# w_q's sixteen-partition block, and the last 128 columns of two weight loads, moved from SyncE's DMA queue to GpSimd's

## The chip, the cores and the metric

The kernel runs on one core of a Trainium2 chip. The metric is the device time of one launch in microseconds. It is the median of several runs; the kernel before has 376.38 us (three runs, 376.34 to 377.0).

## The reference, cut to what matters

One decode step for two rows of x (448 wide). The row is normalised; an attention branch with a cached K and V (8 key-value heads, 16 query heads, 4096 positions of 256) and a feed-forward branch read the normalised row; the second gates the first.

```python
xn = _layernorm(x)                                  # x: 2 x 1 x 448
q = xn @ wq                                         # 448 x 4096
p = softmax(q @ k.T * 256 ** -0.5)                  # k, v: 2 x 8 x 4096 x 256
s = (p @ v) @ wo                                    # wo: 4096 x 448
h = (xn @ w_gate) * (xn @ w_up)                     # 448 x 1792 each
return x + s * silu(h @ w_down)                     # w_down: 1792 x 448
```

Everything is float32. The caches and the weights are some 158 MB, and each byte is used once.

## The kernel before, in words

The kernel is one long stream of loads with the arithmetic beside it. `plan()` (L82) lists the loads in order and `issue()` (L62) sends the next ones. All of them go through SyncE's queue (L75, L79), in this order: `wq0` (half of w_q, 128 partitions x 6656 columns), its extra block `wqx`, `first` (K of the first of 16 batch-head pairs), then fourteen loads `vk[i]` of 8 MB (V of pair i and K of pair i + 1), and among them three loads of weights: `wgu` (w_gate and w_up, 12544 columns) after vk[0], `wdq` (w_down and the other half of w_q, 13440 columns) after vk[2], and `wo` after vk[8]. The last pair's loads `last0` and `last1` are cut into ten pieces. K and V share a ring of two buffers, and all weights one buffer (`slot`), so a load's issue waits until the matmuls that read the buffer's former contents are done.

`wqx` stands for a part of w_q that the kernel takes out of the regular fold. w_q has 448 rows: three blocks of 128 and 64 more. For `wq0` half of those last 64 rows' columns lie on partitions 64 to 127 of the regular load; the other half, 256 KB, is `wqx`: 16 partitions x 4096 columns, read from an array whose outer dimension is 4 (`wqx[:, :4]`, L79; L413 to L415). In `rows()` (L165), which computes x @ w, L173 multiplies the three full blocks, L179 the sixteen-partition block, and L182 or L186 the rest. `query(h)` (L191) turns the result into qT.

Ahead of the first query x is loaded by one DMA of ScalarE's queue (L102), VectorE normalises it (L114 to L124) with one power by GpSimd (L120), TensorE transposes it (L127, L138) with an identity that GpSimd has made.

For each pair, `scores(i)` (L245) multiplies q by K; `softmax` and `over` (L246 to L270) make the transposed weights; `values(i)` (L277) multiplies them by V. The order is written by hand (the pool's scheduler is off): values(i), scores(i + 1), then the issue of the next loads, then the softmax. The feed-forward part (`ffn_in`, L213; `ffn_out`, L223), the second query and the projection by wo (`project`, L301) are put in after pairs 0, 2, 4 and 8. At the end `project_last` (L307) multiplies the last pieces of wo, which come behind the last V in `last1`, and L380 to L382 gate, add and store.

Of the kernel before, what the change touches and what calls it, by code (L numbers as in the profile page):

```python
# [13 lines left out]
B, D = 2, 448  # L14
# [6 lines left out]
FC = F // NT  # L21
KB = 16
ROW = 8192
# [5 lines left out]
PART = 14 * (D + 512)  # L29
SIDE = 16  # L30
EXTRA = 8
EPS = 1e-5


# [2 lines left out]


@with_exitstack
def gated_decode_block(ctx: ExitStack, tc: tile.TileContext, x, first, vk, last0, last1, wq0, wqx, wdq, wo, wgu, out):  # L40
    nc = tc.nc
    ring = ctx.enter_context(tc.tile_pool(name="ring", bufs=2))
    slot = ctx.enter_context(tc.tile_pool(name="slot", bufs=1))
# [5 lines left out]
    def bank(name="t", bufs=1):  # L49
        return psum.tile([128, 512], F32, name=name, bufs=bufs)  # L50
# [8 lines left out]
    loaded = {}  # L59
    todo = []  # L60

    def issue(n=1):  # L62
        for names, src, cuts in todo[:n]:
            weight = names[0].startswith("w")
            if weight:
                t = slot.tile([128, PART], F32, name="slot", align_bytes=512)
            else:
                t = ring.tile([128, 2 * ROW], F32, name="ring", align_bytes=512)
            width = ROW if not weight else src.shape[1] // len(names)
            for i, name in enumerate(names):  # L70
                loaded[name] = t[:, i * width:(i + 1) * width]
            if names == ["wd", "wq1"]:
                loaded["wd"], loaded["wq1"] = t[:, :14 * D], t[:, 14 * D:]
            for lo, hi in zip(cuts, cuts[1:]):
                nc.sync.dma_start(t[:, lo:hi], src[:, lo:hi])  # L75
            if names == ["wq0"]:
                at = src.shape[1]
                loaded["wqx"] = t[:, at:at + EXTRA * 512]
                nc.sync.dma_start(loaded["wqx"][:SIDE], wqx[:, :4])  # L79
        del todo[:n]  # L80

    def plan(names, src, cuts=None):  # L82
# [9 lines left out]
    plan(f"k{LAST + 1} v{LAST}", last0, [0, ROW, 2 * ROW])  # L92
    plan(f"v{LAST + 1} wo2", last1, [0, 4096, 7168, *(ROW + i * D // 2 for i in (0, 6, 12, 14, 15, 16))])
    issue(3)


# [2 lines left out]

    e0, e1 = early()  # L100
    x2 = e0[:, 0, :D]
    nc.scalar.dma_start(x2, x)  # L102
    ident = const.tile([128, 128], F32)
    make_identity(nc, ident)
    one = const.tile([1, 1], F32)
# [11 lines left out]
    nc.vector.scalar_tensor_tensor(sq, xc, 1.0, xc, op0=OP.mult, op1=OP.mult, accum_out=st[:, 2:3])  # L117
    nc.vector.tensor_scalar(st[:, 3:4], st[:, 2:3], 1.0 / D, EPS, op0=OP.mult, op1=OP.add)
    rstd = const.tile([B, 1], F32)
# [16 lines left out]
    for j in range(NK):  # L136
        at = 384 + j * SIDE
# [65 lines left out]
    def lift(ps):  # L203
        t = work.tile([128, D], F32, name="h")
        nc.scalar.copy(t, ps[:, :D])
        return t
# [42 lines left out]
    def softmax(s, m, pT=None):  # L249
        sm = bank("sm", 1)  # L250
        nc.tensor.transpose(sm[:1, :128], m[:, 0:1], ident)  # L251
        mx = work.tile([1, NT, W], F32, name="mx", bufs=1)
        nc.vector.tensor_reduce(  # L253
            mx, sm[:1, None, :128].rearrange("p o (c j) -> p o j c", c=NT).to_broadcast([1, NT, W, NT]),
            axis=AX.X, op=OP.max)
        nc.tensor.transpose(sm[:, 128:129], mx.rearrange("p c j -> p (c j)"), one)  # L256
        nc.vector.tensor_scalar(m[:, 1:2], sm[:, 128:129], -1.0 / 16, None, op0=OP.mult)  # L257
        su = work.tile([128, 2], F32, name="su")
        p = work.tile([128, 2, 512], F32, name="p", bufs=1)
        nc.scalar.activation(p, s, AF.Exp, bias=m[:, 1:2], scale=1.0 / 16, accum_out=su[:, 0:1])  # L260
        if pT is None:
            pT = work.tile([128, 2, 512], F32, name="pT", bufs=1)
        nc.vector.transpose(pT.rearrange("p h n -> p (h n)"), p.rearrange("p h n -> p (h n)"))  # L263
        return pT, su, sm

    def over(p):

        pT, su, sm = p
        nc.tensor.matmul(sm[:, 130:131], add_head.rearrange("p a r j -> p (a r j)"), su[:, 0:1], start=True, stop=True)  # L269
        nc.vector.reciprocal(su[:, 1:2], sm[:, 130:131])  # L270
        return pT, su[:, 1:2]
# [48 lines left out]
    oT2 = const.tile([128, 1, 2, REP, W], F32)  # L320
    ss = scores(0)
    issue(2)
    p = over(softmax(*ss))
    for i in range(LAST):
        g, b = divmod(i, B)
        o = bank("o", 1)
        values(i, p[0], o)
        ss = scores(i + 1)

        issue(1 + (i + 1 in weights))  # L330
        nc.scalar.activation(ob[:, b * 4 + g if g < 4 else b * 3 + g - 4], o, AF.Copy, scale=p[1])  # L331
        if i == LAST - 1:
            cb = combine(ob, 6)
        p = softmax(*ss)
        if i < LAST - 1:
            p = over(p)
        if i == 7:
            cb = combine(ob, 8)
            for n in range(B):
                turn(oT0, cb[:, n * 256:(n + 1) * 256], 0, n, 4)  # L340
            ob = work.tile([128, 8, 512], F32, name="ob", bufs=1)
        if i in (0, 2, 4, 8):
            if i == 0:
                ffn_in()
            if i == 2:
                ffn_out()
            if i == 4:
                query(1)
            if i == 8:
                project(oT0, 0, 0, EARLY)  # L350
# [6 lines left out]
    t = lift(wide)  # L357

    last = slot.tile([128, PART], F32, name="slot", align_bytes=512)
    p = softmax(*ss, last[:, :1024].rearrange("p (h n) -> p h n", h=2))  # L360
    o = bank("o", 1)
# [5 lines left out]
    o = bank("wide", 1)  # L367
# [66 lines left out]
```

## Time and profile before

| what | value |
|---|---|
| median of 3 runs | 376.38 us (376.34 to 377.0) |
| the profiled execution's own time | 376.44 us |
| its span, first to last instruction | 374.7 us |
| TensorE matmul busy | 209.0 us (56% of the span) |
| VectorE, ScalarE, GpSimd busy | 63.2, 36.3, 1.2 us |
| bytes moved by DMA | 158.79 MB, 424 GB/s over the span |

The profile is of one execution. Its lines give start and length in us from the span's start. A load's line stands at its issue on SyncE's queue ("SPq") and not where its bytes move; the share of DMA is the mean over the core's 16 DMA engines. [...] A share can be a few hundredths above 1, since a packet is counted where it starts.

### The profile page before, as it was taken

What the parts mean: (1) busy time and instruction counts of PE and PEld (TensorE: products, weight loads), DVE (VectorE), ACT (ScalarE), POOL (GpSimd) and SP (SyncE); (2) the same over time, 40 slices, a digit from 0 to 9 for tenths busy, and PEclk for the clock granted to TensorE, in tenths of its full rate; (3) what the DMA queues carried; (4) which work ended last, traced back from release to release, by engine and by line L of the source; (5) the groups of instructions that cost most, each with busy time, mean ns of one, the idle gap of its engine ahead of it and who ended that gap; (6) DMA issues with size and microseconds to landing.
All of it is one profiled execution on the core that took longest, in us unless ns stands there. A gap on an engine that the chain in (4) does not pass through costs nothing.

```text
span 374.7 us, 3272 instructions
## 1 busy us (share of the span) xinstructions
PE 209.0 (56%) x1472; PEld 63.0 (17%) x1472; DVE 63.2 (17%) x113; ACT 36.3 (10%) x56; POOL 1.2 (0%) x7
## 2 busy tenths in 40 slices
PE   1792468174736092869174666641718191909795
PEld 0110112021211020212021112210202020202232
DVE  4003021103030003030303030300211203020431
ACT  1001010001012002010101010100010101010120
POOL 1000000000000000000000000000000000000000
PEclk9968586657686567789758687865968776877899
DMA  8999899999999999999999999999999999999994
GB/s 322 438 500 434 374 439 448 441 443 435 425 429 448 441 441 393 429 448 436 427 448 434 436 422 409 444 448 434 441 428 429 441 441 406 450 409 434 415 418 181
DMA packets 4357, 158.79 MB, mean 424 GB/s; under 512 B 614, under 2 KB 1000, under 8 KB 1384
## 3 DMA queue, kind: packets, MB, share of 16 engines
q1 hardware_dynamic: 4340, 158.59, 98.2%
q8 instruction: 11, 0.18, 0.2%
q10 hardware_dynamic: 4, 0.00, 0.0%
q14 instruction: 2, 0.02, 0.0%
HBM read 158.54 MB, written 0.06 MB: 423 GB/s over the span
## 4 chain that ended last, share of the span: by engine, by line
DMA 76%; PE 22%; issue 0%; SPq 0%; DVE 0%
DMA ring<-vk 67%; PE o L277 11%; PE s L245 8%; DMA ring<-last 6%; DMA slot<-wq 3%; PE t L179 1%; PE t L173 1%; PE t L182 1%; SPq L75 0%; PE acc L313 0%; DVE qT L195 0%; DVE h L380 0%; DVE h L381 0%
## 5 line engine op out<-in xcount | busy, mean ns | idle before, releaser
L277 PE MATMUL o<-ring,pT 128*32 128x512 f32 x480 | 83.1, 855 | 91.5 <-DMA ring<-vk 91.5
L245 PE MATMUL s<-ring,qT 128*32 128x512 f32 x512 | 61.8, 624 | 2.4 <-ACT p L260 1.5
L246 DVE TENSOR_REDUCE m<-s 128x1 f32<-128x1024 f32 x16 | 19.6, 1225 | 222.1 <-PE s L245 222.1
L277 PEld LDWEIGHTS o<-ring,pT 128*32 128x32 f32 x480 | 21.2, 149 | 143.6 <-issue 142.0
L331 ACT ACTIVATE ob<-o,su 128x512 f32<-128x512 f32 x14 | 9.6, 688 | 190.7 <-PE o L277 190.7
L260 ACT ACTIVATE p<-s,m 128x1024 f32<-128x1024 f32 x16 | 17.8, 1114 | 97.5 <-DVE m L257 97.5
L245 PEld LDWEIGHTS s<-ring,qT 128*32 128x32 f32 x512 | 18.0, 115 | 44.6 <-issue 40.4
L263 DVE STREAM_TRANSPOSE pT<-p 128x1024 f32<-128x1024 f32 x15 | 18.7, 1245 | 21.2 <-ACT p L260 21.2
L269 PE MATMUL sm<-su,add_head 128*128 128x1 f32 x32 | 7.6, 305 | 22.9 <-ACT p L260 22.9
L251 PE MATMUL sm<-ident,m 128*1 128x128 f32 x16 | 4.3, 270 | 18.9 <-DVE m L246 18.8
L253 DVE TENSOR_REDUCE mx<-sm 1x128 f32<-1x512 f32 x16 | 10.8, 678 | 6.3 <-PE sm L251 6.3
L173 PE MATMUL t<-slot,xnT 128*32 128x512 f32 x48 | 8.8, 887 | 3.4 <-DMA slot<-wq 3.4
L269 PEld LDWEIGHTS sm<-su,add_head 128*128 128x128 f32 x32 | 6.2, 242 | 25.4 <-ACT p L260 24.1
L256 PE MATMUL sm<-one,mx 1*128 1x1 f32 x16 | 3.5, 218 | 12.3 <-DVE mx L253 12.3
L304 PE MATMUL wide<-slot,oT 128*32 128x448 f32 x48 | 7.2, 759 | 0.0
L173 PE MATMUL s<-slot,xnT 128*32 128x448 f32 x48 | 7.2, 748 | 0.1
L227 PE MATMUL t<-slot,hT 128*32 128x448 f32 x28 | 5.6, 911 | 2.4 <-DMA slot<-wdq 2.4
L251 PEld LDWEIGHTS sm<-ident,m 128*1 128x1 f32 x16 | 1.3, 79 | 33.0 <-DVE m L246 32.3
L286 PE MATMUL cb<-ob,add_blocks 128*32 128x64 f32 (+2 forms) x64 | 5.6, 475 | 0.8 <-ACT ob L372 0.8
L179 PE MATMUL t<-slot,oT 16*32 16x512 f32 x16 | 5.7, 703 | 0.0
L195 DVE STREAM_TRANSPOSE qT<-t 128x256 f32<-128x256 f32 x4 | 1.6, 428 | 19.8 <-PE t L179 15.2
L256 PEld LDWEIGHTS sm<-one,mx 1*128 1x128 f32 x16 | 2.1, 133 | 15.4 <-DVE mx L253 15.4
(71 smaller groups left out, 54.1 us busy)
## 6 DMA issues: line engine op xcount, KB each, us to landing
ring<-last SPq DMA_DIRECT2D x2, 4096.0 KB, 24.8
slot<-wdq SPq DMA_DIRECT2D x1, 6720.0 KB
slot<-wgu SPq DMA_DIRECT2D x1, 6272.0 KB, 34.3
slot<-wo SPq DMA_DIRECT2D x1, 5376.0 KB, 40.9
ring<-first SPq DMA_DIRECT2D x1, 4096.0 KB, 21.4
slot<-wq SPq DMA_DIRECT2D x1, 3328.0 KB, 10.7
ring<-last SPq DMA_DIRECT2D x1, 2048.0 KB, 14.7
ring<-last SPq DMA_DIRECT2D x1, 1536.0 KB
```

Of the source, the lines that this page charges most:

```text
L173: nc.tensor.matmul(ps[W * c:W * (c + 1), :n], xnT[:, k, :], block(NT * k + c), start=k == 0, stop=False)
L179: nc.tensor.matmul(ps[W * c:W * (c + 1), :n], xeT[:, j, :], extra[:SIDE, at:at + n], start=False, stop=j == NK - 1)
L227: nc.tensor.matmul(ps[W * t:W * (t + 1), :D], hT[:, i], loaded["wd"][:, i * D:(i + 1) * D], start=i < NT, stop=i >= 14 - NT)
L245: nc.tensor.matmul(s[W * c:W * (c + 1), h, :], q[:, d], k[:, h, d, c, :], start=d == 0, stop=d == 1)
L246: nc.vector.tensor_reduce(m[:, 0:1], s, axis=AX.XY, op=OP.max)
L253: nc.vector.tensor_reduce(mx, sm[:1, None, :128].rearrange("p o (c j) -> p o j c", c=NT).to_broadcast([1, NT, W, NT]), axis=AX.X, op=OP.max)
L260: nc.scalar.activation(p, s, AF.Exp, bias=m[:, 1:2], scale=1.0 / 16, accum_out=su[:, 0:1])
L263: nc.vector.transpose(pT.rearrange("p h n -> p (h n)"), p.rearrange("p h n -> p (h n)"))
L269: nc.tensor.matmul(sm[:, 130:131], add_head.rearrange("p a r j -> p (a r j)"), su[:, 0:1], start=True, stop=True)
L277: nc.tensor.matmul(o[W * t:W * (t + 1), :], pT[:, h, at:at + 2 * W:2], loaded[f"v{i}"][:, e * 512:(e + 1) * 512], start=e < NT, stop=e >= ...
L304: nc.tensor.matmul(wide[W * t:W * (t + 1), :D], heads(oT, i, first), loaded["wo"][:, i * D:(i + 1) * D], start=i < NT, stop=i >= LATE - NT)
L331: nc.scalar.activation(ob[:, b * 4 + g if g < 4 else b * 3 + g - 4], o, AF.Copy, scale=p[1])
```

## The change

`wqx` is loaded by GpSimd's queue and not by SyncE's. The arrays `wgu` and `wdq` lose their last 128 columns, which move into an array `ends`; where these two loads are issued, GpSimd's queue loads the 128 columns in six parts, of 17, 17, 17, 19, 29 and 29 partitions. Each row of a part is two pieces of 64 numbers (256 B), which in `ends` lie 16 numbers apart from each other. x is loaded by two DMAs of one row each, still on ScalarE's queue. Nothing else is changed: what is computed, from which buffers, and the order of all other instructions stay.

```diff
+END = 128
+PARTS = [0, 17, 34, 51, 70, 99, 128]
...
-            width = ROW if not weight else src.shape[1] // len(names)
+            width = ROW if not weight else 28 * FC // len(names)
...
             for lo, hi in zip(cuts, cuts[1:]):
                 nc.sync.dma_start(t[:, lo:hi], src[:, lo:hi])
+            if names in (["wg", "wu"], ["wd", "wq1"]):
+                at = src.shape[1]
+                for lo, hi in zip(PARTS, PARTS[1:]):
+                    nc.gpsimd.dma_start(t[lo:hi, at:at + END].rearrange("p (o n) -> p o n", o=2),
+                                        ends[names[0] == "wd", lo:hi, :, :END // 2])
             if names == ["wq0"]:
                 at = src.shape[1]
                 loaded["wqx"] = t[:, at:at + EXTRA * 512]
-                nc.sync.dma_start(loaded["wqx"][:SIDE], wqx[:, :4])
+                nc.gpsimd.dma_start(loaded["wqx"][:SIDE], wqx[:, :4])
...
-    nc.scalar.dma_start(x2, x)
+    for b in range(B):
+        nc.scalar.dma_start(x2[b:b + 1], x[b:b + 1])
...
+    ends = np.zeros((2, 128, 2, END // 2 + 16), np.float32)
+    for i, w in enumerate((wgu, wdq)):
+        ends[i, :, :, :END // 2] = w[:, -END:].reshape(128, 2, END // 2)
+    wgu, wdq = c(wgu[:, :-END]), c(wdq[:, :-END])
```

More of the change, by code (lines that the diff above doesn't have):

```diff
@@ L31, with gated_decode_block @@
 EXTRA = 8
+END = 128
+PARTS = [0, 17, 34, 51, 70, 99, 128]
 EPS = 1e-5
 @with_exitstack
-def gated_decode_block(ctx: ExitStack, tc: tile.TileContext, x, first, vk, last0, last1, wq0, wqx, wdq, wo, wgu, out):
+def gated_decode_block(ctx: ExitStack, tc: tile.TileContext, x, first, vk, last0, last1, wq0, wqx, wdq, wo, wgu, ends, out):
     nc = tc.nc
@@ L423 @@
     wdq = np.concatenate([wd, wq1], 1)
+    ends = np.zeros((2, 128, 2, END // 2 + 16), np.float32)
+    for i, w in enumerate((wgu, wdq)):
+        ends[i, :, :, :END // 2] = w[:, -END:].reshape(128, 2, END // 2)
+    wgu, wdq = c(wgu[:, :-END]), c(wdq[:, :-END])
     nc = bacc.Bacc("TRN2", target_bir_lowering=False, num_devices=1, dynamic_dma_scratch_size=1024)
-    arrays = dict(x=x, first=first, vk=vk, last0=last[0], last1=last[1], wq0=wq0, wqx=wqx, wdq=wdq, wo=wo, wgu=wgu)
+    arrays = dict(x=x, first=first, vk=vk, last0=last[0], last1=last[1], wq0=wq0, wqx=wqx, wdq=wdq, wo=wo, wgu=wgu, ends=ends)
     args = [nc.dram_tensor(n, a.shape, mybir.dt.from_np(a.dtype), kind="ExternalInput").ap()
```

## The prediction, made before the changed kernel was run

> **What bounds the kernel now.** I read the page first: its DMA line, its queues, its chain.
>
> ```profile
> span 374.7 us, 3272 instructions
> DMA  8999899999999999999999999999999999999994
> q1 hardware_dynamic: 4340, 158.59, 98.2%
> q8 instruction: 11, 0.18, 0.2%
> DMA 76%; PE 22%; issue 0%; SPq 0%; DVE 0%
> ```
>
> The 16 DMA engines are busy in every slice but the last, 98.2% of the span with SyncE's queue, q1. So the kernel is a stream of bytes, and the chain names DMA for 76%. The pace of one engine follows: 158.59 MB in 0.982 x 16 x 374.7 = 5887 us is 26.9 GB/s. With all engines full, the time can move in three ways only: a gap in the stream, more or fewer bytes (here none), or a different sharing of the bytes among the 16 engines, for the slowest engine sets the end. The change touches the third, so the next view is the stretch table of the last microseconds (column before the last: the engines' mean busy share).
>
> ```profile
> 367.25:367.75 0.50, 0.50 (x6) 0.00 (x0) 0.00 (x0) 0.00 (x0) 0.00 (x0) 1.00 1.05 406
> 367.75:368.75 1.00, 0.21 (x6) 0.03 (x5) 0.00 (x0) 0.69 (x1) 0.00 (x0) 1.00 0.73 281
> 368.75:369.25 0.50, 0.50 (x28) 0.50 (x32) 0.03 (x1) 0.00 (x0) 0.00 (x0) 1.00 0.66 244
> 369.25:370.25 1.00, 0.53 (x24) 0.32 (x20) 0.22 (x1) 0.00 (x0) 0.00 (x0) 1.00 0.45 165
> 370.25:370.50 0.25, 0.25 (x13) 0.25 (x17) 0.00 (x0) 0.00 (x0) 0.00 (x0) 1.00 0.35 118
> 370.50:370.75 0.25, 0.25 (x20) 0.25 (x15) 0.00 (x0) 0.00 (x0) 0.00 (x0) 1.00 0.15 50
> 370.75:371.00 0.25, 0.25 (x19) 0.17 (x8) 0.00 (x0) 0.00 (x0) 0.00 (x0) 1.00 0.04 14
> ```
>
> All 16 work until about 367.7; then they stop one after another, and 0.35 x 16 = 5 to 6 of them work beyond 370.25, the last to about 370.9. Work left after 367.75 is 0.73 + 0.33 + 0.45 + 0.09 + 0.04 + 0.01 = 1.65 us on all sixteen, so with a perfect sharing it would end at 369.4. **No sharing can gain more than 1.5 us** (0.4%).
>
> Does the end follow the last bytes? The chain's end says so:
>
> ```profile
> 348.98 21.08 DMA ring<-last
> 370.06 0.14 issue
> 370.19 1.45 PE acc L313 x48
> ```
>
> L313 waits for a piece that lands at 370.06 and then runs at its own pace to the end. An earlier landing is followed at once, as far as about 0.6 us: L313 also needs a VectorE transpose, which ends at 369.47.
>
> ```profile
> 369.22 0.25 DVE L296 STREAM_TRANSPOSE oT<-cb 128x64 f32<-128x64 f32 x1 [2.99 <-PE cb L286]
> ```
>
> That transpose hangs on the last V, whose landing moves with the same engines. So I count the stream's end one to one.
>
> **Who is late?** wqx tells of four engines.
>
> ```profile
> 0.74 10.72 DMA slot<-wq
> 2.48 0.44 SPq L75 DMA_DIRECT2D ring<-vk  x1
> SPq L75 <- DMA slot<-wqx: 10.9, 1, 10.9
> ```
>
> wq has landed at 11.46. SyncE, free at 2.92, waits 10.9 us for wqx: landed at 13.8, 2.4 us behind wq. Its 256 KB on all sixteen engines are 16 KB each, 0.61 us; on four they are 64 KB each, 2.43 us. So four engines carry wqx, and start the long stream 2.4 us behind. The other delays are q8's: 0.2% of 16 x 374.7 = 12 us (9 to 15 by the rounding) for 11 packets of 16 KB, **0.8 to 1.4 us each**, where q1 takes 0.61. Of the 5 to 6 late engines at most four are those of wqx; at least two others end within half a microsecond of the last.
>
> **The change part by part.**
>
> *SyncE's two shorter loads.* Each engine carries 8 rows of a 128-row load. Each row loses 512 B, in two loads: 2 x 8 x 512 B / 26.9 GB/s = **0.30 us less on every engine**.
>
> *The twelve parts.* The same 128 KB come back on GpSimd's queue as 256 B pieces. The price of a small piece, from the tail:
>
> ```profile
> DMA packets 627, 1.33 MB, mean 252 GB/s; under 512 B 81, under 2 KB 465, under 8 KB 626
> q1 hardware_dynamic: 626, 1.32, 63.9%
> ```
>
> This is the stretch 366 to 371.3: 0.639 x 16 x 5.3 = 54.2 us for 1.32 MB, which at the pace are 49.1. The 5.1 us left are 8 ns for each of 626 packets. A piece of 256 B is then 9.5 + 8 = 18 ns if it is a packet by itself, 9.5 ns if its neighbours share one. A part of 17 rows is 34 pieces, 0.32 to 0.60 us; 19 rows 0.36 to 0.67; 29 rows 0.55 to 1.02. No row of GpSimd's queue exists before. If a part is spread over all engines it is nothing in balance (8 rows out, 8 in, up to +0.3). If it is on one engine, that engine has the whole price. I take one engine for each part: wqx went to four, which divides its outer counts 16 and 4, and 17, 19 and 29 are divisible by no smaller number. With 4 + 6 + 6 = 16 shares, I take each engine to get one: wqx's four no part, the other twelve one each. Then wqx's four end 0.30 us sooner, eight engines gain 0.02 to 0.30 (19 rows: 0.37), four gain 0.25 to 0.72.
>
> [...]
>
> *The handover.* q8's packets cost 0.2 to 0.8 us over their 0.61: an engine that takes a packet of another queue loses something. For a part on GpSimd's queue I bound this by 0 and 0.8, and take **0.2**: q8's packet is 16 KB, a part only 8.7. For wqx, four rows of 16 KB an engine, the bound is 0 to 4 x 0.8 = 3.2; I take 0.2, as one handover, because GpSimd's first packets run against a queue that is just filling, and keep the upper end as a rival.
>
> *wqx beside wq.* It no longer stands behind wq but beside it, so wq's last rows on the four engines land up to 2.4 us later. L173 waits for them:
>
> ```profile
> 11.60 4.28 PE t L173 x24
> 23.32 0.33 SPq L75 DMA_DIRECT2D slot<-wgu  x1
> SPq L75 <- DMA ring<-vk: 12.6, 1, 12.6
> ```
>
> The query, and with it the issue of wgu at 23.32, slide to 25.8. What hides it: the queue still holds vk[0], whose landing SyncE awaits from 30.24 for 12.6 us, to 42.8. Cover 19.5 us, slide 2.4: nothing. The same cover takes what GpSimd's issue of wqx puts ahead of the identity and of the power at L120 (nearest rows below: 0.79 us for wqx on SyncE; in this trace GpSimd issues none), and x's second DMA (0.53 us on ScalarE):
>
> ```profile
> 0.74 0.53 ACTq L102 DMA_DIRECT2D p<-x  x1
> 1.18 0.79 SPq L79 DMA_DIRECT2D slot<-wqx  x1
> 8.23 0.25 ACT L149 COPY xg<-t 128x112 f32<-128x112 f32 x1 [5.64 <-PE t L146]
> ```
>
> The normalisation's chain is through at 8.2, 3.4 us ahead of L173. SyncE's `first` and vk[0] issue 0.8 us earlier into a queue that is full: no gain.
>
> *The new waits.* GpSimd's first part waits for the weight buffer as SyncE's wgu does, and five parts queue behind it; nothing else is on GpSimd's queue after L120, so nobody waits there. The readers:
>
> ```profile
> 65.67 0.96 PE L186 MATMUL s<-slot,xnT 64*32 64x448 f32 x8
> 66.69 0.33 SPq L75 DMA_DIRECT2D slot<-wdq  x1
> 168.91 1.06 PE L186 MATMUL t<-slot,xnT 64*32 64x512 f32 x8
> ```
>
> wgu's last columns are read by the last L186 at 65.67, 40 us after the parts are issued; wdq's by 168.91, 102 us after 66.69. Six issues even of 2 us each are hidden many times. If this cover were gone, L186 would hold TensorE, not the stream, until the next ring buffer came free late.
>
> **The sum.** Before, the last engine ends at 370.93 at the latest, the late ones that are not wqx's at 370.3 to 370.7. Afterwards: wqx's at 370.63 (+0.2 for a handover: 370.8); the others at 370.5 + 0.30 + 0.2 = 371.0, between 370.3 and 371.9. I take 371.1, since some late engine may be one with 19 or 29 rows: **+0.2 us**. The profiled execution's 376.44 becomes 376.6; it lay 0.06 above the median, so 376.6 stands for the median too. Own range 376.0 to 377.1. About 0.2% (0.75 us) is what a measurement of this kernel can tell from no change.
>
> **The rivals.**
>
> 1. *The crossing of wqx costs per row* (slower). Every 16 KB row of wqx alternates with a row of wq and costs what a q8 packet does, 0.2 to 0.8 more. Four such on engines that are already last: 4 x 0.5 - 0.30 = +1.7 us, **378.1**, up to 379.3. It decides beyond 0.26 us a row (1.05 / 4). For it: q8's row. Against: q1's own packets follow one another at full pace, and a queue with work waiting need not behave as one that wakes up. 18%.
> 2. *wqx goes to other engines than the four* (slower). If GpSimd's shares begin elsewhere, 2.43 us fall on an engine that is late for another reason: 370.5 - 0.30 + 2.43 = 372.6, +1.7, **378.1**; on engines delayed less, +0.7. Nothing in the trace says where GpSimd's shares begin. 10%.
> 3. *Small pieces cost double* (slower). The pieces of 256 B take 36 ns and not 18: 34 of them 1.2 us, the late engine +0.9, with the handover 371.6, +0.7 to +0.9, **377.2**. 7%. [...]
> 4. *wqx lands on the engines that finish first* (faster). From 367.75 to 368.75 a quarter of the engines is done already. 2.43 us there end by 370.4, its former four drop out, and the late others end at 370.3 to 370.7, less 0.30, plus a part if it is shared finely: **375.6 to 376.1**; the bound of all sharing is 374.9. 10%.
> 5. The forecast: the shares move by tenths of a microsecond and mostly cancel. 55%.
>
> **How the numbers follow.** Slower by over 0.2%: 18 + 10 + 7 = 35%. Faster by over 0.2%: 10%. Within 0.2%: 55%. The range takes in both signs' cheaper halves: 375.7 to 378.4.
>
> **What would show it.** In the profile after: GpSimd's queue as a row of its own with some 0.4 MB; q1 with fewer bytes; L173 at up to 14 us; wgu issued near 25.8, and the DMA line full at 20 to 45 us all the same. In the tail's stretch table the busy share should fall more steeply and later, with fewer engines in the 368s idle, and the last packet within 0.5 us of 370.9. wqx landing much later than 13.8, or an end beyond 371.9, speaks for rival 1 or 2; GpSimd's share of time above 0.4 MB at 26.9 GB/s (15 us, 0.25%) plus 16 x 0.2 us prices the handover. The prediction is wrong if the stream has a gap anywhere before 367, or if the number of engines that end late is set by something that I have not seen.

## The result and the profile after

The changed kernel takes 399.24 us (median of four runs, 398.61 to 399.6), beside 376.37 before: 1.0601 times as long, with a 95% interval of 1.0587 to 1.0614. That is **22.9 us slower**. The forecast was 376.6, and the whole range (375.7 to 378.4) misses it. The profiled execution took 399.51 us, its span 397.8 is 23.1 longer than before.

The page of the changed kernel, first its busy line of DMA and its queues:

```profile
span 397.8 us, 3311 instructions
DMA  8999999993699999999909999999999999999995
q1 hardware_dynamic: 4320, 158.20, 93.3%
q0 software_dynamic: 912, 0.42, 0.5%
DMA 45%; issue 35%; PE 17%; POOL 3%; SPq 0%; DVE 0%; POOLq 0%
```

The chain's last line has "issue", a wait that nothing in the profile explains, at 35%, where before it had 0%. Two holes stand in the DMA line, at slices 10 and 11 and at slice 21 of the 40, where the line of before had none. The queue rows give the account. SyncE's q1 takes 0.933 x 397.8 = 371.1 us of each engine, 3.1 more than before, though it moves 0.4 MB less; GpSimd's q0 takes 2.0 us. The rest, with q8's 0.8, is idle: 23.9 us instead of 6.0. So **18 us are an empty stream, and 5 us are a slower one**. They turned out to have different causes.

Where the stream is empty, the stretch table (after PEclk: DMA share, GB/s):

```profile
94.00:98.00 4.00, 0.00 (x0) 0.00 (x0) 0.00 (x0) 0.00 (x0) 0.00 (x0) 0.50 0.14 52
98.00:102.00 4.00, 0.38 (x1) 0.18 (x2) 0.00 (x0) 0.00 (x0) 1.25 (x1) 0.50 0.10 5
200.00:204.00 4.00, 4.00 (x24) 0.95 (x20) 0.45 (x2) 0.00 (x0) 0.00 (x0) 0.51 0.06 20
204.00:211.00 7.00, 5.05 (x49) 1.19 (x39) 1.78 (x2) 0.69 (x1) 0.00 (x0) 1.00 0.43 150
```

Who is waiting there, by TensorE's timeline around the two holes:

```profile
101.62 1.67 PE L194 MATMUL s<-slot,xnT 64*32 64x448 f32 x2 [14.38 <-DMA slot<-ends]
197.76 1.88 PE L194 MATMUL t<-slot,xnT 64*32 64x512 f32 x2 [15.80 <-DMA slot<-ends]
```

L194 is L186 of before, the last matmuls that read the moved columns. Their last groups begin at 101.6 and 197.8; before, they began at 65.7 and 168.9. In the program's order values and scores come behind them, and TensorE sits idle for 14.4 and 15.8 us until the columns land. So nothing frees the ring meanwhile, and SyncE may not issue. The columns are late because of GpSimd's queue, whose timeline for the first six parts is:

```profile
29.21 1.02 POOL L81 DMA_DIRECT2D slot<-ends  x1 [19.02 <-PE t L187]
43.38 0.96 POOL L81 DMA_DIRECT2D slot<-ends  x1 [13.15 <-issue]
56.03 0.95 POOL L81 DMA_DIRECT2D slot<-ends  x1 [11.69 <-issue]
70.87 1.01 POOL L81 DMA_DIRECT2D slot<-ends  x1 [13.89 <-issue]
85.71 1.25 POOL L81 DMA_DIRECT2D slot<-ends  x1 [13.82 <-issue]
98.03 1.25 POOL L81 DMA_DIRECT2D slot<-ends  x1 [11.06 <-issue]
```

Each is busy for 1 us and then nothing happens for 11 to 14, "issue": a wait that no semaphore in the profile explains. The times to landing of the same six, from the issue table one by one:

```profile
slot<-ends POOLq DMA_DIRECT2D x1, 8.5 KB, 13.8
slot<-ends POOLq DMA_DIRECT2D x1, 8.5 KB, 12.3
slot<-ends POOLq DMA_DIRECT2D x1, 8.5 KB, 14.5
slot<-ends POOLq DMA_DIRECT2D x1, 9.5 KB, 14.5
slot<-ends POOLq DMA_DIRECT2D x1, 14.5 KB, 12.0
slot<-ends POOLq DMA_DIRECT2D x1, 14.5 KB, 3.5
```

29.21 + 13.8 = 43.0, and the next part goes at 43.38; 43.38 + 12.3 = 55.7, and the next goes at 56.03; so it goes on. Each part is issued a third of a microsecond after the one before has landed. The sixth, issued into the hole, lands in 3.5 us. The six parts of the second load go the same way: they are issued from 103.70 to 180.47 and land in 12.2 to 18.5 us.

### The profile page after: what moved, and what is told of

Same layout as the page of the kernel before. It is cut to its first block, busy times and chain, and to the rows that moved or that the text cites. A ratio compares the mean times of both kernels' runs of the same rounds, so it can differ in the third digit from the quotient of the medians.

```text
span 397.8 us, 3311 instructions
## 1 busy us (share of the span) xinstructions
PE 215.8 (54%) x1472; PEld 62.0 (16%) x1472; DVE 63.2 (16%) x113; ACT 36.2 (9%) x56; POOL 14.9 (4%) x20
## 4 chain that ended last, share of the span: by engine, by line
DMA 45%; issue 35%; PE 17%; POOL 3%; SPq 0%; DVE 0%; POOLq 0%
DMA ring<-vk 31%; PE o L285 7%; DMA ring<-last 5%; DMA slot<-ends 5%; PE s L253 4%; DMA slot<-wq 3%; POOL slot L81 3%; PE t L187 2%; PE t L181 1%; PE t L190 1%; PE t L194 0%; PE s L194 0%; SPq L77 0%; PE acc L321 0%; DVE h L388 0%
## 5 line engine op out<-in xcount | busy, mean ns | idle before, releaser
L194 PE MATMUL s<-slot,xnT 64*32 64x448 f32 x16 | 5.9, 856 | 32.4 <-DMA slot<-ends 32.4
L277 PE MATMUL sm<-su,add_head 128*128 128x1 f32 x32 | 6.9, 286 | 22.9 <-ACT p L268 22.9
L81 POOL DMA_DIRECT2D slot<-ends x12 | 12.8, 1069 | 158.7 <-issue 135.2
L194 PE MATMUL t<-slot,xnT 64*32 64x512 f32 x8 | 2.9, 711 | 15.8 <-DMA slot<-ends 15.8
L181 PE MATMUL t<-slot,xnT 128*32 128x512 f32 x48 | 9.8, 985 | 1.0 <-DMA slot<-wq 1.0
L181 PE MATMUL s<-slot,xnT 128*32 128x448 f32 x48 | 7.2, 748 | 1.4 <-DMA slot<-wgu 1.4
L187 PE MATMUL t<-slot,oT 16*32 16x512 f32 x16 | 7.5, 950 | 0.0
```

Of the source, the lines that this page charges most:

```text
L81: nc.gpsimd.dma_start(t[lo:hi, at:at + END].rearrange("p (o n) -> p o n", o=2), ends[names[0] == "wd", lo:hi, :, :END // 2])
L181: nc.tensor.matmul(ps[W * c:W * (c + 1), :n], xnT[:, k, :], block(NT * k + c), start=k == 0, stop=False)
L187: nc.tensor.matmul(ps[W * c:W * (c + 1), :n], xeT[:, j, :], extra[:SIDE, at:at + n], start=False, stop=j == NK - 1)
L194: nc.tensor.matmul(ps[W * c:W * (c + 1), :n], xnT[half, 3, :], block(12 + c % 2)[half], start=False, stop=True)
```

## The experiments

The theories at the start: A, the parts go one after another, either because the room that the kernel sets with `dynamic_dma_scratch_size` (the expectations call it descriptor room) does not hold two (A1) or because GpSimd's queue is always so (A2). A1 counts the room in places and takes a part to need one for each of its pieces and one for its completion; that count is my supposition. The others are B, wqx's crossing costs the time (the prediction's rival 1); C, small pieces are slow in themselves (rival 3).

**e1_wqx_only.** wqx alone on GpSimd's queue, with x in two DMAs; wgu and wdq whole.

```diff
-            if names in (["wg", "wu"], ["wd", "wq1"]):
-                at = src.shape[1]
-                for lo, hi in zip(PARTS, PARTS[1:]):
-                    nc.gpsimd.dma_start(t[lo:hi, at:at + END].rearrange("p (o n) -> p o n", o=2),
-                                        ends[names[0] == "wd", lo:hi, :, :END // 2])
...
-    wgu, wdq = c(wgu[:, :-END]), c(wdq[:, :-END])
```

> wqx on GpSimd's queue and x in two DMAs, as in the changed kernel, but no parts: wgu and wdq are whole on SyncE's queue. Theory A (the 23 us come from the six parts being issued one after another, each when the one before has landed, 13 to 15 us apart): within 0.2% of before, 376.0 to 377.0; L181 starts near 14.0 as in the changed kernel and no stretch of the stream is empty. Theory B (wqx crossing to another queue, the prediction's rival 1): most of the 23 us stays, over 385.

376.41 us, 1.0002 times before (0.9992 to 1.0011). B falls: this half of the change costs nothing that can be measured, and neither do the two DMAs of x. The queue rows of its page:

```profile
q1 hardware_dynamic: 4320, 158.33, 98.1%
q0 software_dynamic: 80, 0.26, 0.2%
```

80 packets are 16 engines x 5, though wqx has only 16 rows. That count is needed below.

**e2_room_for_two.** The changed kernel with more room, 1536 bytes in place of 1024.

```diff
-dynamic_dma_scratch_size=1024
+dynamic_dma_scratch_size=1536
```

> [...] A part of 17 rows has 34 pieces and one completion, 35 places; one of 19 rows 39; one of 29 rows 59. Theory A1 (a part waits for room among the descriptors): two small parts go out together, 70 of 95, and the third waits for the first; the issues in the trace come at 29, 30, 43, 44 and so on; wgu's last part lands near 75 instead of 101; time 377 to 384. Theory A2 (GpSimd's DMAs are one at a time whatever the room is): the same 13 to 15 us between all issues and 399.

387.01 us (1.0274, 1.0237 to 1.0311), three above the expected band, and wgu's last part lands at 97.7 instead of near 75. But what waits for what is as A1 has it. GpSimd's timeline:

```profile
28.67 1.97 POOL L81 DMA_DIRECT2D slot<-ends  x2 [18.41 <-PE t L187]
42.97 0.97 POOL L81 DMA_DIRECT2D slot<-ends  x1 [12.33 <-issue]
49.87 1.00 POOL L81 DMA_DIRECT2D slot<-ends  x1 [5.93 <-issue]
64.98 1.26 POOL L81 DMA_DIRECT2D slot<-ends  x1 [14.11 <-issue]
79.98 1.24 POOL L81 DMA_DIRECT2D slot<-ends  x1 [13.75 <-issue]
```

Two go at once and the third waits for the first. In A1's places 35 + 35 fit and 105 don't. When the first has gone, the third fits; when the second has gone, the fourth (35 + 39). The fifth needs 59 and finds 39 taken, 98 in all, so it waits until all is empty, and so does the sixth; the expectation's dates had left this out. So the room of 1536 bytes is between 74 and 97 of these places; no run shows the expectation's 95 more closely. A2 falls.

**e3_room_for_four.** Still more room, 3072 bytes; the second `h` buffer pays for it.

```diff
-dynamic_dma_scratch_size=1024
+dynamic_dma_scratch_size=3072
...
-        g = work.tile([128, FC], F32, name="h")
-        nc.scalar.copy(g, pp[:, 0, :FC])
-        h = work.tile([128, FC], F32, name="h")
-        nc.vector.tensor_mul(h, pp[:, 1, :FC], g)
+        h = work.tile([128, FC], F32, name="h", bufs=1)
+        nc.scalar.copy(h, pp[:, 0, :FC])
+        nc.vector.tensor_mul(h, pp[:, 1, :FC], h)
...
```

> [...] Theory A1: the first four parts, 35 + 35 + 35 + 39 = 144 places, go out within 5 us, the fifth and sixth wait about 13 us each or less; the last lands before 65.7, where L194 reads it; no empty stretch; 376.0 to 377.0, with the tail shared as the prediction had it (its sum: 376.6). Theory A2: 399.

380.91 us (1.0123, 1.0106 to 1.0140): most of the loss is gone, but 4.6 us stay, which A1 did not expect. GpSimd's timeline, and then the issue table of the first, third, fourth, fifth and sixth part:

```profile
28.95 3.92 POOL L81 DMA_DIRECT2D slot<-ends  x4 [18.39 <-PE t L187]
43.28 1.25 POOL L81 DMA_DIRECT2D slot<-ends  x1 [10.41 <-issue]
57.51 1.24 POOL L81 DMA_DIRECT2D slot<-ends  x1 [12.97 <-issue]
```

```profile
slot<-ends POOLq DMA_DIRECT2D x1, 8.5 KB, 14.0
slot<-ends POOLq DMA_DIRECT2D x1, 8.5 KB, 26.3
slot<-ends POOLq DMA_DIRECT2D x1, 9.5 KB, 32.8
slot<-ends POOLq DMA_DIRECT2D x1, 14.5 KB, 34.1
slot<-ends POOLq DMA_DIRECT2D x1, 14.5 KB, 30.1
```

The issues fit the counting: four parts are 144 places; the fifth (203) waits for the first, landed at 43.0, and with 168 it goes; the sixth with the second gone would make 35 + 39 + 59 + 59 = 192, and it goes at 57.51, right after the third landed (30.9 + 26.3 = 57.2) and not when the second did, near 49.5. So the room of 3072 bytes is between 168 and 191 places. But parts issued together don't land together. By their issue and time to landing these five land at 43, 57, 65, 77 and 88: some 7 us for each small part, 10 to 13 for a large one. The columns are still late at L194:

```profile
87.70 1.67 PE L194 MATMUL s<-slot,xnT 64*32 64x448 f32 x2 [20.02 <-DMA slot<-ends]
```

Does this wait hold the 4.6 us? The page's queue row says no:

```profile
q1 hardware_dynamic: 4320, 158.20, 97.8%
q0 software_dynamic: 912, 0.42, 0.5%
```

0.978 x 379.0 = 370.7 us are busy with q1, 2.7 more than before, and q0 takes 1.9. The stream is full and slow. So a second cause was open.

**e4_one_part.** All 128 rows as one part.

```diff
-PARTS = [0, 17, 34, 51, 70, 99, 128]
+PARTS = [0, 128]
```

> The changed kernel with the 128 columns of each load as one part of 128 rows (16 pieces and one completion for each engine). Theory A: one landing of some 14 us for each load and nothing behind it, so no stall: 376.0 to 377.0; no change in the sharing among engines. Theory C (the small pieces themselves are slow wherever they run, the prediction's rival 3, or a part's own landing is too late): a landing far over 15 us and a time over 380.

376.44 us (1.0004, 0.9994 to 1.0013). The same bytes, in the same 256 B pieces, on the same queue, cost nothing that can be measured as two DMAs (by the interval, from 0.2 us less to 0.5 us more); they land in 10.2 and 9.1 us, where 14 were expected. C falls. Its queue row:

```profile
q0 software_dynamic: 144, 0.39, 0.3%
```

Beside wqx's 80 that is 32 packets for each DMA, two for each of 16 engines. Half of them are under 512 B (the page has 706, and e1's 674): I read one of data and a small one for the completion on each engine. Now the changed kernel's 912: 832 for twelve parts. The stretch 29 to 44 of its trace holds one small part:

```profile
q0 software_dynamic: 64, 0.01, 0.6%
```

64 is 16 x 4. Six parts of 17 rows and two of 19 at 64, and four of 29 rows at 80 (16 x 5), are 832. So **a part puts packets on all sixteen engines**: as many as its pieces need at 16 a packet, e4's number (34 pieces: 3; 58: 4), and a completion. The bytes agree: 0.42 MB is 0.03 more than in e4, which over 15 engines x 512 pieces is some 4 B for each. By these counts an engine without rows of the part gets small packets in place of data. The sizes on the pages say the same, first e1, then the changed kernel, whose GpSimd queue differs by the twelve parts alone:

```profile
DMA packets 4417, 158.79 MB, mean 424 GB/s; under 512 B 674, under 2 KB 1060, under 8 KB 1444
DMA packets 5249, 158.82 MB, mean 399 GB/s; under 512 B 1466, under 2 KB 1860, under 8 KB 2276
```

Of 832 more packets 792 are under 512 B. The other 40 are 8 x 3 + 4 x 4, the data packets of one engine for each part; the 792 are 15 x 40 small ones on the other engines and 12 x 16 completions. Of the 40, 8 are under 2 KB and 32 under 8 KB, as 16 pieces a packet have it: the last 2 or 6 pieces of a small part, and the rest. So by the counts each part's data do lie on one engine, as the prediction took it.

That gave theory F: each visit of GpSimd's queue to an engine costs the stream something, whoever waits. And it would explain the landings: if a visit takes its turn behind a packet of q1, 2.4 us for 64 KB at the 26.9 GB/s of before, three turns are 7.3 us and four 9.7, near the 7 and the 10 to 13 of e3. The next four runs test both.

**e5_cut_before and e6_cut_after.** In both kernels the loads in question are cut, so that a packet of q1 is 16 KB and its turn, at the same pace, 0.61 us.

```diff
-        plan(f"v{i} k{i + 1}", vk[i])
+        plan(f"v{i} k{i + 1}", vk[i], [j * 4096 for j in range(5)] if i < 6 else None)
...
-            plan(*weights[i])
+            plan(*weights[i], [*(j * 4096 for j in range(3)), weights[i][1].shape[1]] if i < 8 else None)
```

> The control for the next run: the kernel before, with the first six loads of 8 MB cut into four pieces of 4096 columns and wgu and wdq into three, so that a row's packet is 16 KB and not up to 64 KB. A packet has some 8 ns of its own: 3 more for each of 8 rows in six loads and 2 in two are 1.4 us at most. All theories: 376.3 to 378.5.

> The changed kernel with the same cuts and its 1024 bytes of descriptor room, so its parts are still one at a time. Theory D (a GpSimd DMA lands late because on each engine it waits its turn behind five or six packets of SyncE's, 2.42 us each at 64 KB): with packets of 16 KB (0.61 us) a part lands in 4 to 6 us instead of 13 to 15, six of them in 25 to 36 us, before or near L194's reading; the time within 0.5% of the control's. Theory E (a part's 13 to 15 us are GpSimd's or the piece's own, whatever runs beside it): still 13 to 15 us and a time over 395.

The control took 377.42 us, the changed kernel 381.78, 4.4 more: over the half percent that D allowed, and far under E's 395. The issue table of e6, the first part and the fourth:

```profile
slot<-ends POOLq DMA_DIRECT2D x1, 8.5 KB, 8.9
slot<-ends POOLq DMA_DIRECT2D x1, 9.5 KB, 7.4
```

A part lands in 7.4 to 8.9 us instead of 12 to 14.5. E falls. D holds in kind: the landing depends on the packets that run beside it. It misses in size: the difference is some 6 us for 1.8 us a packet, which is three turns, and some 6 us don't depend on the packet. e4's two landings, 10.2 and 9.1 us with one data packet on an engine, are near 6 + 2.4. What the 6 us are was not tried. The 4.4 us are F's: L194 still waits, but no hole stands in e6's DMA line, and q1 and q0 together are busy for 4.4 us more than q1 in the control (372.0 + 1.9 against 369.5).

**e7_late_before and e8_late_after.** The cover is made longer and the parts stay as they are.

```diff
-    weights = {0: ("wg wu", wgu), 2: ("wd wq1", wdq), 8: ("wo", wo)}
+    weights = {0: ("wg wu", wgu), 4: ("wd wq1", wdq), 8: ("wo", wo)}
...
-        if i in (0, 2, 4, 8):
-            if i == 0:
+        if i in (2, 5, 6, 8):
+            if i == 2:
                 ffn_in()
-            if i == 2:
+            if i == 5:
                 ffn_out()
-            if i == 4:
+            if i == 6:
                 query(1)
```

> The control for the next run: the kernel before with the feed-forward's first half after pair 2 (not 0), wdq's load after vk[4] (not vk[2]), the second half after pair 5 (not 2) and the second query after pair 6 (not 4). The same work in another order: 376.0 to 377.5 by all theories.

> The changed kernel in the same later order, with its 1024 bytes of descriptor room. Its parts stay 13 to 15 us apart, but wgu's columns are now read near 110 and wdq's near 205. Theory A: with the cover back the stalls are gone: 376.0 to 377.5, within 0.3% of the control, and the tail shows what the new sharing is worth (the prediction's sum: +0.2 us). Theory F (the parts cost the stream something else as well, in turns or in engine time): 1% or more over the control.

376.36 us for the control (0.9993, 0.9983 to 1.0002) and 380.91 for the changed kernel (1.0115, 1.0098 to 1.0132). The 18 us of stall are gone, though the parts are still 12 to 18 us apart: no L194 waits for a DMA any more. But 4.5 us stay. Its queue rows:

```profile
q1 hardware_dynamic: 4320, 158.20, 97.7%
q0 software_dynamic: 912, 0.42, 0.5%
```

0.977 x 378.9 = 370.2 us for q1 and 1.9 for q0, together 4.1 more than the 368.0 of before; the span is 4.2 longer. The pace of q1 fell from 26.9 to 26.7 GB/s an engine. Theory A alone had 376.0 to 377.5; that is missed, and F's 1% is borne out.

**e9_late_half and e10_late_room.** Half the parts in the later order; and all of them with room for four (and one h buffer, as in e3), so that all land long before they are read.

```diff
-            if names in (["wg", "wu"], ["wd", "wq1"]):
+            if names == ["wg", "wu"]:
...
-    wgu, wdq = c(wgu[:, :-END]), c(wdq[:, :-END])
+    wgu = c(wgu[:, :-END])
```

```diff
-dynamic_dma_scratch_size=1024
+dynamic_dma_scratch_size=3072
```

> The later order (as e8_late_after), with parts for wgu only; wdq is whole on SyncE's queue. Theory F (each part sends packets through every one of the 16 engines, and each such visit costs the stream something, some 0.35 us a part on every engine): six parts cost half of twelve, 1.8 to 2.6 us over the later order's control, 378.2 to 379.0. Theory G (what is left over in the later order is a stall at the reading of wdq's columns, which are late): the control's time, 376.0 to 377.0.

> The later order with all twelve parts and 3072 bytes of descriptor room (and one h buffer): four parts go out at once and the rest sooner, all have landed long before they are read. Theory F: the cost is of the parts' packets and not of when they go: 380.4 to 381.4 as in e8_late_after. Theory G: without any late landing 376.0 to 377.0.

378.48 us and 381.01 us, beside 376.58 before: +1.9 and +4.4. Six parts cost about half of twelve, and it does not matter when they are issued. G falls, F stands: **0.32 to 0.37 us a part on every engine**, at 4 or 5 packets each. Whether the price goes by the packet or by the piece isn't shown: e4 has 4 packets and 32 pieces of its parts on an engine, where the changed kernel has 52 and 512, and by either count it would pay 0.3 us, inside its interval. By the DMA (two at 0.35) it would pay 0.7, outside it. Why q1 loses pace stays open.

No run beats the kernel before. The two changed kernels that come level (e1, e4) also end as before: from 368 to 369 us the engines' mean busy share is 0.78 and 0.73, beside 0.75.

## Why the prediction was wrong

**"Six issues even of 2 us each are hidden many times" failed.** This step makes 18 of the 23 us. It counted what GpSimd is busy with (1 us a part, well within the 2 allowed), and put the wait between two issues at nothing without a reason. The parts' own order, "five parts queue behind it", was seen, but only asked for who else stands on that queue; the queue's own waits were not asked for. The cover was sized nearly rightly: 36 us from the first issue to the reading of before, where 40 were forecast. The chain that had to fit was six landings one after another, 72 us (29.21 to 101.5). A gap in the stream before 367, which the prediction named as a sign of its being wrong, is what came. The kernel's line with 1024 bytes of descriptor room was there to be read. No row of before gave a price for GpSimd's queue, and that is where an unknown wait should have been bounded upwards, by one landing for each part. The bound was at hand: wqx on SyncE's queue landed 12.6 us after its issue, and six times that does not fit in 40.

**"If it is on one engine, that engine has the whole price" failed.** It makes the other 5 us. The data do go in few packets, but every engine carries packets of every part. One engine for each part was an estimate of mine, from wqx's four. What the other fifteen get is shown by the counts above: of the 64 packets of a part of 17 or 19 rows 3 are its data, 45 are small ones in place of data, and 16, one for each engine, are left for the completion. That each engine gets one part, as the sum had it, no run shows.

**The handover, "take 0.2" for each part on its engine**, was mis-sized in its reach rather than its height: 0.35 a part, on sixteen engines instead of one. Twelve of them add up on each engine, where I had one on each.

**wqx** held: nothing in balance (e1). Rivals 1 and 3, 18% and 7%, were wrong by e1 and e4. Rivals 2 and 4 are not seen either: in e1, with wqx on GpSimd's queue, the time is that of before. Which engines then carried wqx the profile doesn't tell.

**The slide at the start** was hidden, as said, but longer: wgu issued at 28.93 instead of the 25.8 forecast. L181 did start at 14.03. Behind it TensorE's granted clock was 0.50 in the stretch 24 to 29, while the query was still running, and its last twelve matmuls of L187 took 5.33 us, where they had taken 3.60.

```profile
24.00:29.00 5.00, 4.89 (x12) 0.72 (x8) 0.06 (x1) 0.00 (x0) 0.00 (x0) 0.50 0.97 419
```

x came later than the 0.5 us that I gave its second DMA. In VectorE's timeline the first instruction on x starts at 7.45, where it had started at 2.61:

```profile
7.45 0.61 DVE L122 TENSOR_REDUCE st<-p 2x1 f32<-2x448 f32 x1 [6.56 <-DMA p<-x]
```

That is 4.8 us and passes the cover of 3.4; wq's own delay hid the rest. The second issue ended only 0.2 us later than the one of before (1.48, 1.27), so the row was held up after it; whether by wq's packets or by wqx's no run separates.

**The sharing**, the heart of the forecast, moved by no more than can be seen, so its +0.2 us is neither shown nor refuted. The steeper fall that the prediction named as its sign did not come. The tail of e8, with its stall gone, against its control e7's:

```profile
372.00:373.00 1.00, 0.21 (x13) 0.15 (x15) 0.00 (x0) 0.69 (x1) 0.00 (x0) 1.00 0.75 289
373.00:374.00 1.00, 0.85 (x40) 0.61 (x33) 0.25 (x1) 0.00 (x0) 0.00 (x0) 1.00 0.61 227
374.00:374.50 0.50, 0.17 (x8) 0.20 (x12) 0.00 (x0) 0.00 (x0) 0.00 (x0) 1.00 0.36 126
374.50:375.00 0.50, 0.50 (x28) 0.50 (x24) 0.00 (x0) 0.00 (x0) 0.00 (x0) 1.00 0.16 56
```

```profile
368.00:369.00 1.00, 0.32 (x20) 0.32 (x24) 0.00 (x0) 0.63 (x1) 0.00 (x0) 1.00 0.72 272
369.00:370.00 1.00, 0.69 (x33) 0.45 (x22) 0.25 (x1) 0.00 (x0) 0.00 (x0) 1.00 0.54 198
370.00:370.50 0.50, 0.34 (x16) 0.37 (x20) 0.00 (x0) 0.00 (x0) 0.00 (x0) 1.00 0.30 104
370.50:371.00 0.50, 0.50 (x31) 0.41 (x22) 0.00 (x0) 0.00 (x0) 0.00 (x0) 1.00 0.10 32
```

The engines stop over the same 3 us, in the same staircase. The parts did not even it out; what they were to gain, at most some tenths, is lost in the 4.5 us that they cost. The changed kernel's own tail is steeper (full to 392, empty by 394), but its stream had been empty twice, so it doesn't tell what the parts did. Which engine took which part the profile doesn't tell.

## What to carry to other kernels

Ask of a DMA that is cut into parts three things: what one part has to wait for (here for room on GpSimd's queue: with 1024, 1536 and 3072 bytes one, two and four of the first parts went at once), how long one landing takes beside the stream that runs (here 12 to 18.5 us beside packets of 64 KB), and how many engines each part visits (here all 16, whatever its rows). Multiply the landing by the number of parts before calling it hidden. In this kernel, which is bound by its stream of bytes, an even sharing of the last 3 us (worth at most 1.5 us by the prediction's bound) could not pay for a dozen extra DMAs on a second queue, which cost 4.4.

## What the runs showed of the hardware that I had not expected

- GpSimd's queue held back a part until it fitted beside those not yet landed. Counted as pieces + 1 places a part, one room for each run explains the issue of each of the first six parts in three runs, down to the one that waited at 192: by what went and what waited it lies between 59 and 69 places with 1024 bytes (the changed kernel), 74 and 97 with 1536 (e2), and 168 and 191 with 3072 (e3).
- A part on GpSimd's queue, though its data lie on one engine by the counts, sent packets of up to 16 pieces to every engine: 64 packets for 17 or 19 rows, 80 for 29. The 128 rows in one DMA made 32 packets, with 16 pieces on each engine.
- Each part cost the full stream 0.32 to 0.37 us on every engine (6 parts 1.9 us, 12 parts 4.4), while its bytes are worth 0.02 to 0.03 us an engine.
- How soon a part landed depended on the packets beside it: 12 to 18.5 us at 64 KB a packet, 7.4 to 8.9 at 16 KB (e6), 3.5 in an empty stream.
